# The middle query slot of a head pair: its two 64-query halves alternate, and with float32 scores it becomes one product

## The chip, the cores and the metric

The kernel runs on one NeuronCore of one Trainium2 chip. The metric is device time in microseconds (us) of one execution; of the kernel before, three runs are known: 794.02, 794.14 and 795.17 us, median 794.14 us. One more execution was taken by the hardware profiler, and everything said here of stretches, waits and instructions comes from that trace.

## The reference

Attention over 4 batches, 8 heads, 576 positions and head dimension 64, followed by a token-mixing block and a gated block on the result seen as (4, 576, 512):

```
scores = q @ k.T / 8                     # per batch and head, 576 x 576
scores = where(scores >= rowmax - tau, scores, -1e9)
attn   = softmax(scores)
x      = attn @ v                        # heads side by side: (4, 576, 512)
u      = x + (relu(x.T @ w_tok1) @ w_tok2).T
x      = u + relu(u @ w_ch1) @ w_ch2
h      = relu(x @ w_in);  c = conv3(h) along the sequence
out    = (h * sigmoid(c)) @ w_out
```

## The kernel before, in words

The heads are taken in pairs, `NP` = 4 pairs in each of the four batches. The two heads of a pair lie on the two halves of the 128 partitions: head 0's 64 head dimensions on partitions 0 to 63, head 1's on 64 to 127. The 576 queries of a head are four blocks of 128 and a rest of 64, so a pair has `NSL` = 9 slots of 128 queries: slots 0 to 3 are head 0's blocks, slots 5 to 8 head 1's, and slot 4, the middle one, holds the last 64 queries of both heads. `cut(slot)` says so: for the middle slot it gives two parts of 64 output partitions each, (0, 64, head 0) and (64, 64, head 1); for every other slot one part of 128.

`prep` loads a pair, `scores` makes a slot's scores on TensorE (PE) into one of two or three PSUM places, `exps`, `mask`, `ph` and `rest` run the row maximum, the exponential, the threshold and the split into a high and a low float16 half on VectorE (DVE), ScalarE (ACT) and GpSimd (POOL), a DMA transpose issued from SyncE (SP) turns the probabilities, and `pv` multiplies them with the values: per part nine key blocks `j`, each with the high half of v, and for `j` up to 4 also with the low half, hence 14 products of 65 or 64 columns per part. The middle slot has two parts, so 28 products, and in them only 64 of the 128 array columns are used (the profile writes 128*64).

The scores come in two kinds. In batches 0 and 1 (`NB32` = 2) they are float32 products: the queries `qt` stand as weights, and the keys stream through. There are two key tiles per pair, `kt[0]` and `kt[1]`, each with zeros on the other head's partitions, so that the contraction over 128 partitions sees one head. A slot is two products of 288 columns (the halves `a` of the keys); the middle slot is four, two for each head. In batches 2 and 3 the scores are float16 products of split operands, two passes `x` for each `a`.

The work is written as generators that step in turn: `attention(b + 1)` is woven between the products of `dense(b)` (token mixing is `tok`; L547, L565, L598, L621 and L624 are the dense products). Batch 0's attention has nothing dense to lie beside. A scheduler that runs when the program is built then places the instructions of every engine in a fixed order, by its own estimate of durations, so an edit can move instructions far from it. Each engine, and the SP queue of DMA issues, works through its own order and waits at semaphores.

Names in the rows: `ps` is PSUM, `pt` and `act_t` hold the transposed probabilities, `vh` and `vl` the halves of v, `wc`, `wi`, `wo` weights, `st` staged weights, `ld` loaded v.

Of the kernel before, what the change touches and what calls it, by code (L numbers as in the profile page):

```python
# [9 lines left out]
F16 = mybir.dt.float16  # L10
# [9 lines left out]
def kernel(ctx: ExitStack, tc: tile.TileContext, q, k, v, tau,  # L20
# [7 lines left out]
    nc = tc.nc  # L28
    B, NPR, _, S = q.shape
    H, D = 2 * NPR, 64  # L30
    P = 128
# [7 lines left out]
    NS = S // P  # L39
    R0 = NS * P  # L40
    SPL = [(0, 256), (256, S - 256)]
    NB32 = 2
# [12 lines left out]
    const = ctx.enter_context(tc.tile_pool(name="const", bufs=1))  # L55
# [10 lines left out]
    V, A, G, T = nc.vector, nc.scalar, nc.gpsimd, nc.tensor  # L66
# [41 lines left out]
    def hold(x):  # L108
        return tc.issue_after(turn[behind[x]].ins) if behind.get(x) in turn else nullcontext()
# [93 lines left out]
    for t in h_t:  # L203
# [2 lines left out]
    v_t = [(const.tile([P, 2, 2 * NS + 1, D + 2], F16, name=f"vh{i}"),  # L206
            const.tile([P, 2, NS + 1, D], F16, name=f"vl{i}")) for i in range(2)]
    qk_t = [(const.tile([P, 2, S], F16, name=f"qt{i}"),
             [const.tile([P, 2, S], F16, name=f"kt{i}_{h}") for h in range(2)]) for i in range(2)]

    def f32(t):
        return t.rearrange("p a s -> p (a s)").bitcast(F32)
# [10 lines left out]
    NSL = 2 * NS + 1  # L223

    def split(out, t, sc):
        A.activation(out=out[:, 0], in_=t, func=AF.Copy, scale=sc)
        V.scalar_tensor_tensor(out=out[:, 1], in0=t, scalar=sc, in1=out[:, 0], op0=ALU.mult, op1=ALU.subtract)

    def prep(b, p):

        vh, vl = v_t[p % 2]
        qt, kt = qk_t[p % 2]
        pair[b, p] = dict(qt=qt, kt=kt, vh=vh, vl=vl)
        if b < NB32:
            with hold("qk") if b else nullcontext():
                nc.sync.dma_start(f32(qt), q[b, p])
                for h in range(2):
                    if b == 0 and p < 2:
                        G.memset(f32(kt[h])[(1 - h) * D:(2 - h) * D], 0.0)
                    nc.sync.dma_start(f32(kt[h])[h * D:(h + 1) * D], k[b, p, h * D:(h + 1) * D])  # L240
            if b:
                yield
                yield
            A.activation(out=f32(qt), in_=f32(qt), func=AF.Copy, scale=qsc[:, 0:1])
        else:
            qn, kn = [qk2.tile([P, S], F32, tag="x", name="ld", bufs=15) for _ in range(2)]
            with hold("qk"):
                nc.sync.dma_start(qn, q[b, p])
                nc.sync.dma_start(kn, k[b, p])
        if b >= NB32:  # L250
            yield
            qs = qk2.tile([P, 2, S], F16, tag="x", name="qs", bufs=15)
            split(qs, qn, qsc[:, 1:2])
            for h in range(2):
                for x in range(2):
                    nc.sync.dma_start(qt[x * D:(x + 1) * D, h], qs[h * D:(h + 1) * D, x])
            yield
            ks = qk2.tile([P, 2, S], F16, tag="x", name="ks", bufs=15)
            split(ks, kn, QK)
            for h in range(2):  # L260
                for r in range(2):
                    nc.sync.dma_start(kt[h][r * D:(r + 1) * D], ks[h * D:(h + 1) * D])
        yield
        vn = []
        for hh in range(2):
            t = qk2.tile([P, S], F32, tag="x", name="ld", bufs=15)
            with hold("qk") if b else nullcontext():
                nc.sync.dma_start(t, v[b, 2 * p + hh])
            vn.append(t.rearrange("p (a d) -> p a d", d=D))
        yield  # L270
        for hh in range(2):
            G.tensor_scalar(out=vn[hh], in0=vn[hh], scalar1=VSC, scalar2=1.0, op0=ALU.mult, op1=ALU.mult)
            A.activation(out=vh[:, hh, :, 0:D], in_=vn[hh], func=AF.Copy)
            G.tensor_tensor(out=vl[:, hh], in0=vn[hh][:, 0:NS + 1], in1=vh[:, hh, 0:NS + 1, 0:D], op=ALU.subtract)
            yield

    def cut(slot):

        if slot == NS:
            return [(0, 64, 0, R0), (64, 64, 1, R0)]  # L280
        return [(0, P, 0, slot * P) if slot < NS else (0, P, 1, (slot - NS - 1) * P)]
# [4 lines left out]
    pair, chk, done = {}, {}, set()  # L286
    ps = psum.tile([P, 8, 512], F32, name="ps")
    hn = S // 2
# [8 lines left out]
    def where(i):  # L297
        return i // PER, i // NSL % NP, i % NSL

    def scores(i):  # L300
        b, p, slot = where(i)
        st = pair[b, p]
        o2 = 2 * (i % 3 if i < PER else i % 2)
        s3 = ps[:, o2:o2 + 2, :hn]
        for o, m, hh, q0 in cut(slot):
            for a in range(2):
                if b < NB32:
                    T.matmul(s3[o:o + m, a], f32(st["qt"])[:, q0:q0 + m],  # L308
                             f32(st["kt"][hh])[:, a * hn:(a + 1) * hn], start=True, stop=True)
                    continue  # L310
                for x in range(2):
                    T.matmul(s3[o:o + m, a], st["qt"][:, hh, q0:q0 + m],  # L312
                             st["kt"][hh][:, x, a * hn:(a + 1) * hn], start=(x == 0), stop=(x == 1))
        chk[i] = dict(s3=s3)

    def half(i, x):
# [42 lines left out]
    def pv(i):  # L359
        b, p, slot = where(i)  # L360
        st = pair[b, p]
        vh, vl, pt = st["vh"], st["vl"], chk.pop(i)["pt"]
        n = slot if slot <= NS else slot - NS - 1
        dst = ps[:, 7, n * (D + 1):(n + 1) * (D + 1)]
        for o, m, hh, _ in cut(slot):
            for j in range(NSL):
                T.matmul(dst[o:o + m], pt[:, j, o:o + m], vh[:, hh, j, 0:D + 1],  # L367
                         start=(j == 0), stop=(j == NSL - 1))
                if j <= NS:
                    T.matmul(dst[o:o + m, 0:D], pt[:, j, o:o + m], vl[:, hh, j], start=False, stop=False)  # L370
        if slot == 0:
            st["x32"] = p2.tile([P, NS + 1, P], F32, tag="x32", name="x32", bufs=1)
            st["xp"] = [p2.tile([P, NS + 1, P], F16, tag=f"x{x}", name=f"x{x}") for x in "hl"]
        if slot in (NS, NSL - 1):
            norm(ps[:, 7], st["x32"], st["xp"], 0 if slot == NS else 1)

    def norm(pvt, x32, xp, hh):


        n = NS + 1 - hh  # L380
        p3v = pvt[:, :n * (D + 1)].rearrange("p (a d) -> p a d", d=D + 1)
        rc = sm.tile([P, NS + 1, 1], F32, tag="rc", name="rc")
        V.tensor_scalar(out=rc[:, :n], in0=p3v[:, :, D:D + 1], scalar1=1e-9 * ONE, scalar2=None, op0=ALU.add)
        V.reciprocal(out=rc[:, :n], in_=rc[:, :n])
        cs = slice(hh * D, (hh + 1) * D)
        parts = [(slice(0, NS), cs)]
        V.tensor_tensor(out=x32[:, 0:NS, cs], in0=p3v[:, 0:NS, 0:D],
                        in1=rc[:, 0:NS].to_broadcast([P, NS, D]), op=ALU.mult)
        if hh == 0:
            V.scalar_tensor_tensor(out=x32[:, NS].rearrange("p (h d) -> p h d", h=2),  # L390
                                   in0=p3v[:, NS:NS + 1, 0:D].to_broadcast([P, 2, D]), scalar=rc[:, NS],
                                   in1=blk.to_broadcast([P, 2, D]), op0=ALU.mult, op1=ALU.mult)
            parts.append((slice(NS, NS + 1), slice(0, P)))
        for ss, cc in parts:
            A.activation(out=xp[0][:, ss, cc], in_=x32[:, ss, cc], func=AF.Copy)
            G.tensor_tensor(out=xp[1][:, ss, cc], in0=x32[:, ss, cc], in1=xp[0][:, ss, cc], op=ALU.subtract)
# [54 lines left out]
    def attention(b):  # L451
# [9 lines left out]
        for i in range(c0, c1, NSL):  # L461
            bb, p, _ = where(i + NSL)
            if bb < B:
                start(i - 1, prep(bb, p), (1, 2, 2, 1, 1, 1))
            start(i + NSL - 1 + lag + 2, tok(b, where(i)[1]), (2, 1, 1))
        if b == 0:
            for _ in prep(0, 0):
                pass
        i = c0 - 1
        while i < c1 + lag or todo:  # L470
            if c0 <= i < c1:
                exps(i)
            yield
            if c0 <= i - 1 < c1:
                mask(i - 1)
                ph(i - 1)
                if i == PER:
                    free.append(5)
            yield
            if c0 <= i - lag < c1:  # L480
                pv(i - lag)
            if c0 <= i - 1 < c1:
                rest(i - 1)
            for j in range(i + 1, i + (3 if i + 2 < PER else 2)):
                if j < c1 and j not in done:
                    scores(j)
                    done.add(j)
            yield
            for g in todo.pop(i, ()):
                next(g, None)  # L490
            yield
            i += 1
# [235 lines left out]
```

## Time and profile before

| what | value |
|---|---|
| median of three runs | 794.14 us |
| span of the profiled execution, first to last instruction | 783.1 us |
| what lies around the span (median less span) | 11.0 us |
| PE busy | 731.0 us, 93% of the span |
| DVE / ACT / POOL busy | 493.8 / 471.3 / 423.0 us |
| granted PE clock, mean | 0.997 of full speed |

No time of the profiled execution other than its span is known; the runs' median stands in for it. A busy share of PE counts products that overlap in the array as one busy stretch, so the share alone does not tell how far PE is from its limit; the start of one product to the start of the next does. Rows of the timeline give the start, the duration until the result is out, the shape and a count; consecutive products of one line are merged, and "128*64" means that 64 array columns are in use.

### The profile page before, as it was taken

How to read it: one execution, taken by the hardware profiler on the slowest of the kernel's cores; microseconds unless marked ns; L12 is line 12 of the kernel's file. 1: busy time of each engine (PE TensorE's matmuls, PEld its weight loads, DVE VectorE, ACT ScalarE, POOL GpSimd, SP SyncE). 2: the span in 40 equal slices, each digit the busy share in tenths (PEclk: the TensorE clock that was granted, in tenths of full speed). 3: DMA queues.
4: the chain of work that ended last, by engine and by line, in shares of the span. 5: the costliest groups of instructions: out<-in, count | busy, mean ns of one | idle time of the engine just before them, and what ended most of it. 6: DMA issues, size and time to landing. Idle time of an engine off the chain costs nothing. (4 is left out here: it accounts for less than half of the span.)

```text
span 783.1 us, 18470 instructions
## 1 busy us (share of the span) xinstructions
PE 731.0 (93%) x7388; PEld 554.2 (71%) x7388; DVE 493.8 (63%) x837; ACT 471.3 (60%) x998; POOL 423.0 (54%) x471
## 2 busy tenths in 40 slices
PE   5679978999987899999999999999999999999998
PEld 3457756778766675788887856788888756878764
DVE  5578876877677861666877980676876850323370
ACT  7789967876667762666656852676656741311371
POOL 5988889887786651355664950366564830000040
PEclk9999999999999999999999999999999999999999
DMA  8999998997987421668667412667664401000001
GB/s 282 187 241 189 173 233 190 215 245 204 229 212 171 89 35 42 142 146 159 130 142 156 84 40 76 127 144 156 146 129 76 77 15 48 1 1 2 1 1 61
DMA packets 195046, 97.84 MB, mean 125 GB/s; under 512 B 174096, under 2 KB 176656, under 8 KB 194960
## 3 DMA queue, kind: packets, MB, share of 16 engines
q1 hardware_dynamic: 194640, 96.39, 55.3%
q8 instruction: 58, 0.95, 0.5%
q10 hardware_dynamic: 320, 0.26, 0.1%
q14 instruction: 28, 0.23, 0.1%
HBM read 42.36 MB, written 4.72 MB: 60 GB/s over the span
## 5 line engine op out<-in xcount | busy, mean ns | idle before, releaser
L352 POOL TENSOR_TENSOR ph<-e,ph 128x576 f16<-128x576 f32 x108 | 141.3, 1308 | 94.3 <-ACT ph L348 87.4
L565 PE MATMUL ps<-act_t,wc_h 128*128 128x256 f16 (+1 forms) x768 | 149.0, 286 | 0.0
L324 DVE TENSOR_REDUCE nm<-ps 128x1 f32<-128x576 f32 x144 | 107.9, 752 | 44.1 <-PE ps L312 27.0
L588 POOL TENSOR_TENSOR act_t<-ct,act_t 128x576 f16<-128x576 f32 x32 | 46.6, 1456 | 138.8 <-ACT act_t L587 135.9
L547 PE MATMUL ps<-u_h,wc_h 128*128 128x256 f16 (+1 forms) x384 | 109.7, 286 | 0.8 <-DVE act_t L522 0.8
L565 PE MATMUL ps<-act_t,wc_l 128*128 128x256 f16 (+1 forms) x384 | 109.8, 286 | 0.0
L547 PE MATMUL ps<-u_h,wc_l 128*128 128x256 f16 (+1 forms) x384 | 109.6, 286 | 0.0
L547 PE MATMUL ps<-u_l,wc_h 128*128 128x256 f16 (+1 forms) x384 | 109.2, 286 | 0.0
L308 PE MATMUL ps<-kt,qt 128*128 128x288 f32 (+1 forms) x320 | 87.8, 433 | 18.6 <-DVE act_t L343 9.0
L343 DVE SCALAR_TENSOR_TENSOR e<-ps,thr,e 128x576 f32<-128x576 f32 x108 | 87.8, 813 | 21.1 <-POOL thr L332 9.4
L547 PEld LDWEIGHTS <-wc_h 128*128 128x128 f16 x768 | 75.1, 98 | 19.9 <-issue 1.3
L565 PEld LDWEIGHTS <-wc_h 128*128 128x128 f16 x768 | 74.9, 98 | 19.0 <-issue 0.5
L367 PE MATMUL ps<-vh,pt 128*128 128x65 f16 (+1 forms) x1080 | 71.9, 195 | 8.5 <-DMA pt<-ph 5.8
L598 PE MATMUL ps<-u_h,wi_h 128*128 128x256 f16 (+1 forms) x256 | 73.0, 286 | 6.4 <-ACT h L574 3.3
L583 DVE SCALAR_TENSOR_TENSOR ct<-h,cw,ct 128x576 f32<-128x576 f32 x64 | 68.4, 1069 | 14.8 <-ACT ct L581 14.3
L621 PE MATMUL ps<-wo_h,act_t 128*128 128x512 f16 x256 | 76.3, 379 | 1.5 <-DVE u_l L430 0.9
L367 PEld LDWEIGHTS <-pt 128*128 128x128 f16 (+1 forms) x1080 | 62.4, 101 | 18.3 <-DMA pt<-ph 10.2
L308 PEld LDWEIGHTS ps<-kt,qt 128*128 128x128 f32 (+1 forms) x320 | 50.5, 185 | 33.8 <-DVE act_t L343 12.7
L348 ACT ACTIVATE ph<-e 128x576 f16<-128x576 f32 x108 | 73.0, 676 | 2.1 <-DVE e L343 2.1
L598 PE MATMUL ps<-u_h,wi_l 128*128 128x256 f16 (+1 forms) x256 | 73.1, 286 | 0.0
L598 PE MATMUL ps<-u_l,wi_h 128*128 128x256 f16 (+1 forms) x256 | 73.1, 286 | 0.0
L621 PEld LDWEIGHTS <-act_t 128*128 128x128 f16 x384 | 36.7, 98 | 43.6 <-issue 1.7
(113 smaller groups left out, 1613.0 us busy)
## 6 DMA issues: line engine op xcount, KB each, us to landing
st<-in_moe_w_ch_dram SPq DMA_DIRECT2D x24, 512.0 KB, 4.3
ld<-in_v_dram SPq DMA_DIRECT2D x32, 288.0 KB, 3.6
kt<-ks SPq DMA_DIRECT2D x32, 144.0 KB, 2.7
st<-in_moe_w_in_dram SPq DMA_DIRECT2D x8, 512.0 KB, 4.7
st<-in_moe_w_out_dram SPq DMA_DIRECT2D x8, 512.0 KB, 4.5
out_dram<-ot SPq DMA_DIRECT2D x16, 256.0 KB, 2.0
qt<-in_q_dram SPq DMA_DIRECT2D x8, 288.0 KB, 3.6
kt<-in_k_dram SPq DMA_DIRECT2D x16, 144.0 KB, 3.7
```

Source lines behind the costliest of these rows:

```text
L308: T.matmul(s3[o:o + m, a], f32(st["qt"])[:, q0:q0 + m], f32(st["kt"][hh])[:, a * hn:(a + 1) * hn], start=True, stop=True)
L324: crit["max"] = V.tensor_reduce(out=nm, in_=c["s3"], axis=AX.XY, op=ALU.max, negate=True)
L343: crit["mask"] = V.scalar_tensor_tensor(out=e3, in0=c["s3"], scalar=c["thr"], in1=e3, op0=ALU.is_ge, op1=ALU.mult)
L348: A.activation(out=c["ph"][:, 0:S], in_=c["e"], func=AF.Copy)
L352: G.tensor_tensor(out=c["ph"][:, S:], in0=c["e"], in1=c["ph"][:, 0:S], op=ALU.subtract)
L367: T.matmul(dst[o:o + m], pt[:, j, o:o + m], vh[:, hh, j, 0:D + 1], start=(j == 0), stop=(j == NSL - 1))
L547: T.matmul(t, wc1[wx][:, f, c], u[c][ux][:, sl], start=(c == 0 and i == 0), stop=(c == NC - 1 and i == 2))
L565: T.matmul(t, wc2[wx][:, c, f], r_t(f, rx)[:, sl], start=(by_dve(c) and f == 0 and i == 0), stop=(f == NF - 1 and i == 2))
L583: V.scalar_tensor_tensor(out=ct, in0=ht[:, kk:kk + S], scalar=cw[:, kk, f:f + 1], in1=ct, op0=ALU.mult, op1=ALU.add)
L588: G.tensor_tensor(out=g_t(f, 1), in0=ct, in1=g_t(f, 0), op=ALU.subtract)
L598: T.matmul(t, wi[wx][:, f, c], u[c][ux][:, s0:s0 + n], start=(c == 0 and i == 0), stop=(c == NC - 1 and i == 2))
L621: T.matmul(t, g_t(f, gx)[:, j * P:(j + 1) * P], wo[wx][:, f], **lim)
```

## The change

In the middle slot the products of the two halves alternate: in `pv` the loop over the parts moves inside the loop over `j`, and in the float16 branch of `scores` inside the loops over `a` and `x`. For float32 scores the roles are exchanged: the zeros now lie in two query tiles `kts[:, h]`, held side by side, the keys lie whole in `qt`, and a slot is a window of 128 columns over the two query tiles. Head 1's queries are stored rotated, its last 64 first, so the window of slot 4 covers the last 64 queries of both heads, and the slot is two products of 128 columns instead of four of 64. The rotation makes head 1's query load two DMAs instead of one.

```diff
-             [const.tile([P, 2, S], F16, name=f"kt{i}_{h}") for h in range(2)]) for i in range(2)]
+             const.tile([P, 2, 2, S], F16, name=f"kt{i}")) for i in range(2)]
 ...
             with hold("qk") if b else nullcontext():
-                nc.sync.dma_start(f32(qt), q[b, p])
+                nc.sync.dma_start(f32(qt), k[b, p])
                 for h in range(2):
                     if b == 0 and p < 2:
                         G.memset(f32(kt[h])[(1 - h) * D:(2 - h) * D], 0.0)
-                    nc.sync.dma_start(f32(kt[h])[h * D:(h + 1) * D], k[b, p, h * D:(h + 1) * D])
+                nc.sync.dma_start(f32(kt[0])[0:D], q[b, p, 0:D])
+                nc.sync.dma_start(f32(kt[1])[D:P, S - R0:S], q[b, p, D:P, 0:R0])
+                nc.sync.dma_start(f32(kt[1])[D:P, 0:S - R0], q[b, p, D:P, R0:S])
 ...
-        for o, m, hh, q0 in cut(slot):
+        if b < NB32:
+            qs = f32(st["kts"].rearrange("p h x s -> p (h x) s"))[:, slot * P:(slot + 1) * P]
             for a in range(2):
-                if b < NB32:
-                    T.matmul(s3[o:o + m, a], f32(st["qt"])[:, q0:q0 + m],
-                             f32(st["kt"][hh])[:, a * hn:(a + 1) * hn], start=True, stop=True)
-                    continue
+                T.matmul(s3[:, a], qs, f32(st["qt"])[:, a * hn:(a + 1) * hn], start=True, stop=True)
+        else:
+            for a in range(2):
                 for x in range(2):
-                    T.matmul(s3[o:o + m, a], st["qt"][:, hh, q0:q0 + m],
-                             st["kt"][hh][:, x, a * hn:(a + 1) * hn], start=(x == 0), stop=(x == 1))
+                    for o, m, hh, q0 in cut(slot):
+                        T.matmul(s3[o:o + m, a], st["qt"][:, hh, q0:q0 + m],
+                                 st["kt"][hh][:, x, a * hn:(a + 1) * hn], start=(x == 0), stop=(x == 1))
 ...
-        for o, m, hh, _ in cut(slot):
-            for j in range(NSL):
+        for j in range(NSL):
+            for o, m, hh, _ in cut(slot):
                 T.matmul(dst[o:o + m], pt[:, j, o:o + m], vh[:, hh, j, 0:D + 1],
                          start=(j == 0), stop=(j == NSL - 1))
-                if j <= NS:
+            if j <= NS:
+                for o, m, hh, _ in cut(slot):
                     T.matmul(dst[o:o + m, 0:D], pt[:, j, o:o + m], vl[:, hh, j], start=False, stop=False)
```

The scheduler's order, at three places. First PE, at the `pv` products of the middle slot of batch 0's first pair (before, the point where head 0's part ends and head 1's begins; `vh` high half, `vl` low half):

```order
L367 MATMUL ps<-vh_153,act_t 64x65
L367 LDWEIGHTS act_t
L367 MATMUL ps<-vh_153,act_t 64x65
L367 LDWEIGHTS act_t
L367 MATMUL ps<-vh_153,act_t 64x65
L370 LDWEIGHTS act_t
L370 MATMUL ps<-vl_154,act_t 64x64
```

and the beginning of the same slot now:

```order
L373 LDWEIGHTS act_t
L373 MATMUL ps<-vh_153,act_t 64x65
L373 LDWEIGHTS act_t
L373 MATMUL ps<-vh_153,act_t 64x65
L377 LDWEIGHTS act_t
L377 MATMUL ps<-vl_154,act_t 64x64
L377 LDWEIGHTS act_t
L377 MATMUL ps<-vl_154,act_t 64x64
```

Before, all 14 products of one head stand ahead of the other's 14; now each product of head 0 is followed by head 1's.

Second PE again, at the `pv` products of the middle slot of batch 2's second pair, which lie between dense products (`wc` weights). Before:

```order
L565 MATMUL ps<-act_t,wc_h 128x320
L367 LDWEIGHTS pt
L367 MATMUL ps<-vh_155,pt 64x65
L370 LDWEIGHTS pt
L370 MATMUL ps<-vl_156,pt 64x64
```

and now:

```order
L572 MATMUL ps<-act_t,wc_h 128x320
L373 LDWEIGHTS pt
L373 MATMUL ps<-vh_155,pt 64x65
L318 LDWEIGHTS qt_157
L318 MATMUL ps<-kt_158,qt_157 128x288
L318 LDWEIGHTS qt_157
L318 MATMUL ps<-kt_158,qt_157 128x288
L318 LDWEIGHTS qt_157
L318 MATMUL ps<-kt_158,qt_157 128x288
L318 LDWEIGHTS qt_157
L318 MATMUL ps<-kt_158,qt_157 128x288
L373 LDWEIGHTS pt
```

Here four full-width score products of another slot have moved in behind the first 64-column product, so the slot is visited in two pieces. Over the whole program the `pv` products of middle slots stand in 21 pieces before and in 25 now, the float16 middle scores in 10 before and 11 now, and the 8 float32 ones in 8 before and in none now.

Third SP, the queue of DMA issues, from the v loads at the start of the program. Before:

```order
L268 DMA ld<-in_v_dram 128x576 x8
L357 DMA_TRANSPOSE act_t<-act_t 128x9x128
L118 DMA st<-in_moe_w_tok_dram 128x576 x2
L357 DMA_TRANSPOSE act_t<-act_t 128x9x128
L240 DMA kt_0_158<-in_k_dram 64x576
L236 DMA qt_157<-in_q_dram 128x576
L357 DMA_TRANSPOSE act_t<-act_t 128x9x128
```

and now:

```order
L273 DMA ld<-in_v_dram 128x576 x8
L243 DMA kt_158<-in_q_dram 64x576
L118 DMA st<-in_moe_w_tok_dram 128x576
L363 DMA_TRANSPOSE act_t<-act_t 128x9x128
L118 DMA st<-in_moe_w_tok_dram 128x576
L363 DMA_TRANSPOSE act_t<-act_t 128x9x128 x2
L118 DMA st<-in_moe_w_tok_dram 128x576
L239 DMA qt_157<-in_k_dram 128x576
L244 DMA kt_158<-in_q_dram 64x512
L245 DMA kt_158<-in_q_dram 64x64
```

The third pair's first load, which waits for PE's scores of the first pair's middle slot, has moved ahead of the first transpose, and the load that waits for the first pair's last slot has moved behind the third. Each of the eight float32 pairs has one load more. From batch 2 on SP's order of loads and transposes is the same as before.

## Rows read from the trace of the kernel before

**Rows 1.** Windows: busy us (count) of PE, PEld, DVE, ACT, POOL; clock, DMA share, GB/s.

```profile
0.00:125.00 125.00, 96.23 (x1082) 72.10 (x1083) 92.83 (x180) 101.00 (x217) 100.99 (x117) 0.99 0.98 220
125.00:280.00 155.00, 140.13 (x1409) 108.98 (x1409) 118.70 (x199) 112.50 (x236) 122.64 (x130) 1.00 0.80 186
280.00:620.00 340.00, 337.23 (x3634) 261.67 (x3633) 225.83 (x367) 204.38 (x439) 176.01 (x209) 1.00 0.54 113
```

**Rows 2.** Windows of 20 us, the same columns.

```profile
440.00:460.00 20.00, 18.40 (x252) 15.57 (x252) 18.43 (x25) 15.31 (x34) 17.24 (x16) 1.00 0.45 69
620.00:640.00 20.00, 18.43 (x192) 12.55 (x191) 14.58 (x19) 12.08 (x24) 9.74 (x9) 1.00 0.14 27
```

**Rows 3.** Waits of PE from 125 to 280 us: total us, times, longest.

```profile
PE ps L367 <- DMA pt<-ph: 3.1, 5, 1.0
```

**Rows 4.** Timeline of PE, one middle slot's pv products and what follows.

```profile
353.30 0.22 PE L367 MATMUL ps<-vh,pt 128*64 128x65 f16 x1
353.35 0.20 PE L370 MATMUL ps<-vl,pt 128*64 128x64 f16 x1
...
353.64 0.23 PE L367 MATMUL ps<-vh,pt 128*64 128x65 f16 x3
353.70 0.20 PE L370 MATMUL ps<-vl,pt 128*64 128x64 f16 x1
353.70 0.23 PE L367 MATMUL ps<-vh,pt 128*64 128x65 f16 x3
353.76 0.20 PE L370 MATMUL ps<-vl,pt 128*64 128x64 f16 x1
...
353.98 0.29 PE L367 MATMUL ps<-vh,pt 128*64 128x65 f16 x4
354.21 0.28 PE L547 MATMUL ps<-u_h,wc_h 128*128 128x256 f16 x1
354.32 0.27 PE L547 MATMUL ps<-u_h,wc_l 128*128 128x256 f16 x1
```

**Rows 5.** Timeline of PE, the output projection's 48 half-width products.

```profile
311.65 0.41 PE L624 MATMUL ps<-wo_h,act_t 128*64 128x256 f16 x4
...
314.19 0.28 PE L624 MATMUL ps<-wo_l,act_t 128*64 128x256 f16 x2
```

**Rows 6.** Timeline of PE, float32 scores: three whole slots, then a middle slot.

```profile
66.86 3.15 PE L308 MATMUL ps<-kt,qt 128*128 128x288 f32 x12
69.85 0.19 PE L367 MATMUL ps<-vh,act_t 128*128 128x65 f16 x1
...
150.44 1.20 PE L308 MATMUL ps<-kt,qt 128*64 128x288 f32 x8
151.56 0.31 PE L547 MATMUL ps<-u_h,wc_h 128*128 128x320 f16 x1
```

**Rows 7.** Timeline of PE, a middle slot's float16 scores.

```profile
358.60 0.69 PE L312 MATMUL ps<-kt,qt 128*64 128x288 f16 x8
359.22 0.28 PE L547 MATMUL ps<-u_h,wc_l 128*128 128x256 f16 x1
```

**Rows 8.** Timeline of PE, a piece of two half-width products between whole ones.

```profile
173.28 0.30 PE L547 MATMUL ps<-u_l,wc_h 128*128 128x320 f16 x1
173.51 0.25 PE L367 MATMUL ps<-vh,pt 128*64 128x65 f16 x2
173.69 0.99 PE L308 MATMUL ps<-kt,qt 128*128 128x288 f32 x3
```

**Rows 9.** Timeline of SP: start and duration of DMA issues.

```profile
15.35 1.65 SPq L357 DMA_TRANSPOSE act_t<-act_t  x1
...
20.88 0.55 SPq L240 DMA_DIRECT2D kt<-in_k_dram  x1
24.46 0.34 SPq L236 DMA_DIRECT2D qt<-in_q_dram  x1
```

**Rows 10.** Waits of SP's queue from 15 to 125 us: total us, times, longest.

```profile
SPq L357 <- POOL act_t L352: 14.0, 13, 2.4
```

More of the change, by code (lines that the diff above doesn't have):

```diff
@@ L231, in prep @@
         vh, vl = v_t[p % 2]
-        qt, kt = qk_t[p % 2]
-        pair[b, p] = dict(qt=qt, kt=kt, vh=vh, vl=vl)
+        qt, kts = qk_t[p % 2]
+        kt = [kts[:, h] for h in range(2)]
+        pair[b, p] = dict(qt=qt, kt=kt, kts=kts, vh=vh, vl=vl)
         if b < NB32:
             with hold("qk") if b else nullcontext():
-                nc.sync.dma_start(f32(qt), q[b, p])
+                nc.sync.dma_start(f32(qt), k[b, p])
                 for h in range(2):
```

## The prediction

> **What bounds the kernel now.** I read the windows first, to see where PE is the limit. Up to 125 us, batch 0's attention, PE is busy 96.2 of 125 us, while the DMA engines stand at a share of 0.98 and ACT and POOL at 101 us each: PE is not the limit. From 125 to 280 us (batch 1's attention inside the first dense block) PE is busy 140.1 of 155 us, with POOL at 122.6: mixed. From 280 to 620 us (batches 2 and 3's attention inside the dense blocks) PE is busy 337.2 of 340 us, and no other engine passes 226: there a product less is time less [rows 1]. Two stretches near this one are exceptions: from 440 to 460 and from 620 to 640 us PE is busy 18.4 of 20 us [rows 2], so the middle slots there, one of batch 2 and the last of batch 3, save little. That leaves six of the eight middle slots of these batches on a full PE. After 640 us the attention is over and nothing changes.
>
> Then I read the timeline of PE at the places that the diff touches, for the step from start to start, since a busy share hides how products overlap.
>
> **The pv products.** In one middle slot head 0's first ten steps take 0.29 us after the second start (353.35 to 353.64, nine steps), 0.032 us each. The slot is 28 products and runs from 353.30 to the next product at 354.21, 0.91 us; the row at 353.98 holds the last four, so the last starts at about 354.08, 0.78 us after the first. In one place the two heads overlap: where head 0 ends and head 1 begins, eight starts fall between 353.64 and 353.76, 0.12 us, 0.017 us a step [rows 4]. So the engine does run the two halves of the array beside each other, but only for the few products that it sees at the border. What alternation does is in the trace too: the output projection's half-width products (L624) already alternate. 46 of them start in 2.54 us (311.65 to 314.19), 0.110 us a pair [rows 5], and a full-width product of 256 columns also steps by 0.11 us (354.21 to 354.32) [rows 4]. So a pair of halves costs what one costs. For pv this makes 14 pairs: 0.05 us for the first step and 12 times 0.032, 0.43 us from first to last start in place of 0.78. The saving is 0.35 us a slot. Bounds: 0.35 by rows 5; by the border's 0.017 us, 27 steps are 0.46 and the saving is 0.32; if the overlap doesn't last, none. I take 0.35, the row with a sustained alternation.
>
> A rule speaks against it. The Trainium skill, "TensorE: Matmul & The Clock Gate", section "Wait — 56ns, not 53.3ns?", says that start-to-start never falls below about 25 ns however few columns a matmul has. By it a slot would be 27 times 0.025, an estimate of 0.68 us, the saving 0.1, and the whole sum about 793.4 us. The 0.017 us at the border [rows 4] lies under that floor, so I give the rule's case less weight than the forecast; it stands beside the rival "no overlap".
>
> **The float32 middle score.** Three whole slots of four instructions take 2.99 us to the next product (66.86 to 69.85), 1.00 us each. The middle slot, eight half-width instructions, takes 1.12 us (150.44 to 151.56) [rows 6]: its halves overlap already, and half the instructions are not half the time. What is left is the visit: going from whole to half-width and back. A piece of two half-width products stands between a product at 173.28 and one at 173.69, 0.41 us, of which about 0.13 is the step of the first and 0.06 the two products: a visit costs 0.22 us [rows 8]. The middle slot's 0.12 us holds the way back, and the way in adds about 0.1. I take 0.2 us saved per slot (bounds 0.12 and 0.22), four in batch 0 and four in batch 1.
>
> **The float16 middle score.** Eight products take 0.62 us to the next [rows 7]. They overlap too. If the second head starts when the first is two products ahead at most, alternation saves some 0.03 us; I take 0.03 (bounds 0 and 0.1), eight slots, 0.24 us.
>
> **More pieces.** The order now visits the half-width products in more pieces. On the full PE it is three more: two pv slots of batches 2 and 3 whose first product stands alone ahead of four whole score products, and one float16 score. At 0.22 us they give back 0.66 us. In batch 1 it is one more, 0.22 us.
>
> **The loads.** A pair with float32 scores has four loads for three. An issue stands 0.55 us on SP's queue at 20.88 us [rows 9], so eight pairs cost between nothing, if SP has time, and 8 times 0.55, 4.4 us, if SP paces the stage; six of the eight lie in the first 125 us, 3.3 us. The third pair's first load now stands ahead of the first transpose (15.35 us) and waits for PE's middle score; behind it are the transposes, and behind these pv's first products. In return the load that went out at 24.46 us, held by PE's last slot, no longer stands ahead of the third transpose. The bytes are the same. SP's own longest sum of waits here is for POOL, 14.0 us in 13 waits [rows 10], so SP is mostly not the pacer, and I take little: 1 us lost in batch 0. The same stage has PE savings of 4 times 0.35 and 4 times 0.2, 2.2 us, behind other engines; I take 1 us of it, and the stage's sum is 0, between 2.2 us less and 3.3 us more. The copy that scales the tile, the clears of the zero halves and the number of scaled elements stay as they were.
>
> **The sum.** Batches 2 and 3: six times 0.35 is 2.1, and 0.24, less 0.66: 1.7 us saved. Batch 1: four times 0.35 and four times 0.2, less 0.22, is 2.0 us of PE work. PE has 15 us idle of 155 there, and five of its waits, 3.1 us, are for the transposes that feed these very slots [rows 3], so a shorter slot often only lengthens the next wait; I take half, 1.0 us (bounds 0 and 2.0). Batch 0: 0. Together 2.7 us. The span of the profiled execution, 783.1 us, becomes 780.4; the 11.0 us around it stay, which gives 791.4 us against the median of 794.14.
>
> **The rivals.**
>
> *No overlap in pv.* Products of 65 columns may be handed out too fast to keep both halves fed, and a slot stays at 0.78 us. For it: the overlap at the border lasts only eight starts, and the sustained one is of products four times as long. Against: those eight starts. Then batches 2 and 3 lose 0.66 less 0.24, 0.4 us, batch 1 wins half of 0.8 less 0.22, 0.3: 794.2 us, no change.
>
> *The whole saving passes.* Batch 1's PE work counts in full (2.0) and batch 0's too (2.2, no load in the way), with 1.7: 5.9 us, 788.2 us. For it: the float32 scores feed the row maximum that frees the next PSUM place, so a shorter PE slot shortens that circle. Against: POOL and the DMA engines at rows 1.
>
> *SP paces the first 280 us.* Place: SP's queue, with one load more per pair and one ahead of the first transpose. Price: eight loads at 0.55, 4.4 us, and 0.55 us more ahead of the first transpose, 5.0 us; the transposes come later by as much, so batch 1's saving turns into waits for them. With 1.7 us won later it is 3.3 us slower: 797.4 us. It decides from 3.3 us lost, six loads, on. For it: the DMA share of 0.98; against: SP's waits for POOL.
>
> **How the numbers follow.** Forecast 0.56 (its own range 789.6 to 793.2), whole saving 0.14, no overlap 0.17, SP 0.13. A measurement of this kernel tells no change from one of 0.2%, 1.6 us: below 792.55 is faster, above 795.7 slower. The forecast's own range lies 0.83 below the line: 0.46, and with 0.14 that gives faster 0.60. The rest of the forecast, 0.10, and 0.16 of "no overlap" are the same, 0.26. SP's 0.13 and 0.01 from the middle cases are slower, 0.14. The scheduler has moved rows in all the first 280 us, and no row prices this; the range takes it in: 788.0 us, the whole saving, to 795.3, past "no overlap" and a third of the way to SP's case.
>
> **What would show it.** In the changed profile a middle slot's pv products should run 0.45 us or less from first to last start, in pairs of starts a few ns apart, and no float32 score row should be 128*64, each slot at 1.00 us. Right: PE still full from 280 to 620 us, the end of batch 3's attention earlier by about 2.7 us, and the time to the end of batch 0's attention within 1 us of before. Wrong: a pv slot at 0.7 us or more (the handing out binds); the first transpose 2 us later and never caught up (SP); or PE idle where it was full, the saving turned into waits for transposes or DVE.

## The result, and the profile after

The changed kernel takes 802.63 us (median of 4 runs, 801.55 to 805.6) against 794.52 us for the kernel before on the same chip: ratio 1.0129, 95% interval 1.0099 to 1.0159. It is slower; the forecast was 791.4 us, its range ended at 795.3. (The two medians alone give 1.0102; here and below the ratio is the recorded one, with its interval.)

First a correction to the table ahead of the prediction. In every later profile a run's time is its span and 1.8 us (after: 803.8 and 805.6). By that the profiled execution of before, with a span of 783.1 us, was one of some 785 us and lay at the fast end: before's runs in the experiments go from 784.58 to 795.36. Of the 11.0 us "around the span" only 1.8 are there. No term of the sum hangs on them, but stage times of that one profile are early by several us, so a second profile of before (first experiment, span 792.0) stands beside it below.

What the diff does in PE's products came out as worked out. In the timeline of the changed kernel, a middle slot's `pv` products and what follows, as in [rows 4]:

```profile
374.17 0.22 PE L373 MATMUL ps<-vh,pt 128*64 128x65 f16 x2
374.22 0.20 PE L377 MATMUL ps<-vl,pt 128*64 128x64 f16 x2
374.25 0.20 PE L373 MATMUL ps<-vh,pt 128*64 128x65 f16 x2
...
374.51 0.29 PE L373 MATMUL ps<-vh,pt 128*64 128x65 f16 x8
374.73 0.28 PE L554 MATMUL ps<-u_h,wc_h 128*128 128x256 f16 x1
374.85 0.27 PE L554 MATMUL ps<-u_h,wc_l 128*128 128x256 f16 x1
```

The halves start in pairs (x2). From the first product to the dense product behind the slot it is 0.56 us (374.17 to 374.73) where it was 0.91: 0.35 us less, the forecast's number. From first to last start seven of the nine undivided slots of 28 take 437 to 439 ns (780 to 782 in all of before's). The other two take 488 and 730 ns; PE is at half clock in part of the first and in all of the second.

The float32 middle slot is now a whole slot, 1.05 us from start to next (before 1.12, [rows 6]), and the float16 one takes 0.62 us as before [rows 7]:

```profile
150.93 1.21 PE L313 MATMUL ps<-qt,kt 128*128 128x288 f32 x4
151.98 0.30 PE L554 MATMUL ps<-u_h,wc_h 128*128 128x320 f16 x1
...
379.12 0.68 PE L318 MATMUL ps<-kt,qt 128*64 128x288 f16 x8
379.74 0.28 PE L554 MATMUL ps<-u_h,wc_l 128*128 128x256 f16 x1
```

The loss is elsewhere. SP's timeline of the changed kernel, to be held against [rows 9]:

```profile
9.63 7.78 SPq L273 DMA_DIRECT2D ld<-in_v_dram  x8
17.51 0.47 SPq L243 DMA_DIRECT2D kt<-in_q_dram  x1
18.09 0.52 SPq L118 DMA_DIRECT2D st<-in_moe_w_tok_dram  x1
18.70 1.61 SPq L363 DMA_TRANSPOSE act_t<-act_t  x1
```

The first transpose is issued at 18.70 us, before at 15.35 (16.19 in the second profile). Four more issues stand ahead of it: one more query load in each of the first two pairs, the third pair's first load, and a weight load. The windows of [rows 1] now:

```profile
0.00:125.00 125.00, 93.28 (x988) 69.82 (x989) 87.25 (x170) 94.34 (x203) 95.16 (x110) 0.90 0.98 202
125.00:280.00 155.00, 137.74 (x1324) 106.19 (x1323) 108.90 (x188) 104.55 (x218) 113.49 (x124) 0.98 0.82 193
280.00:620.00 340.00, 330.27 (x3520) 252.70 (x3519) 224.34 (x363) 200.76 (x433) 174.72 (x207) 0.99 0.56 112
```

In the first 125 us all engines do less than in [rows 1] (ACT 94.34 us for 101.00, POOL 95.16 for 100.99), and PE's mean granted clock is 0.90 of full speed for 0.99. But the second profile of before does hardly more in that window, so most of this difference is spread between executions of one kernel:

```profile
0.00:125.00 125.00, 93.03 (x1021) 68.91 (x1022) 89.00 (x173) 96.66 (x206) 96.40 (x112) 0.96 0.98 209
125.00:280.00 155.00, 142.25 (x1378) 110.21 (x1377) 115.13 (x193) 111.29 (x230) 121.35 (x129) 0.97 0.83 191
```

From 125 to 280 us the changed kernel's engines are behind both profiles of before, and its third window is less full because batch 1's stage now reaches into it. Its waits of PE for transposes (total us, times, longest), up to 125 us and from 125 to 280 us:

```profile
PE ps L373 <- DMA act_t<-act_t: 11.2, 11, 4.4
...
PE ps L373 <- DMA pt<-ph: 5.7, 8, 1.9
```

In the second profile of before the first of these rows is:

```profile
PE ps L367 <- DMA act_t<-act_t: 10.8, 11, 2.1
```

So up to 125 us the total is hardly larger than in that execution of before; what is new is one wait of 4.4 us, to which the end of the section on the experiments comes back. From 125 to 280 us the total is 5.7 us for 3.1 and 2.8 in the two profiles of before, so there the transposes come late, as a rival foresaw. But with the order kept, the fastest kernel of all, it is 4.6 us: these sums do not show what the waits cost.

By stages, us from the span's start to the first dense product and then by dense block, read from starts of products. A block ends at the start of its last whole product of the output projection (L621 before); block 0 holds batch 1's attention, block 1 batch 2's, block 2 batch 3's. It is one execution each: the same kernel differs by 4 us in the first two columns, so only the experiments' medians decide. The profiles of the changed kernel and the second one of before are of the slowest of their runs, 805.6 and 793.8 us.

| kernel | first dense product | block 0 | block 1 | block 2 | PE at half clock |
|---|---|---|---|---|---|
| before, profile given | 114.3 | 197.1 | 172.7 | 173.2 | 3.4 |
| before, second profile | 118.6 | 201.6 | 172.8 | 173.1 | 20.4 |
| after | 124.4 | 208.0 | 174.0 | 172.0 | 37.4 |
| order kept, halves alternate | 115.7 | 200.6 | 171.3 | 172.0 | 13.6 |
| new order, halves alternate | 118.6 | 205.7 | 173.2 | 173.8 | 23.8 |
| new order, halves in turn | 119.2 | 203.7 | 174.2 | 173.2 | 17.0 |

### The profile page after: what moved, and what is told of

It reads as the page before. It is cut to its first block, busy times and chain, and to the rows that moved or that the text cites. A ratio compares the mean times of both kernels' runs of the same rounds, so it can differ in the third digit from the quotient of the medians.

```text
span 803.8 us, 18420 instructions
## 1 busy us (share of the span) xinstructions
PE 739.5 (92%) x7356; PEld 557.8 (69%) x7356; DVE 496.0 (62%) x837; ACT 470.0 (58%) x998; POOL 422.7 (53%) x471
## 5 line engine op out<-in xcount | busy, mean ns | idle before, releaser
L313 PE MATMUL ps<-qt,kt 128*128 128x288 f32 x288 | 94.3, 460 | 22.8 <-DVE e L349 8.4
L554 PE MATMUL ps<-u_h,wc_h 128*128 128x320 f16 (+1 forms) x384 | 109.3, 286 | 0.3 <-DVE act_t L529 0.3
L554 PE MATMUL ps<-u_h,wc_l 128*128 128x320 f16 (+1 forms) x384 | 109.5, 286 | 0.0
L554 PE MATMUL ps<-u_l,wc_h 128*128 128x320 f16 (+1 forms) x384 | 108.7, 286 | 0.0
L313 PEld LDWEIGHTS ps<-qt,kt 128*128 128x128 f32 x288 | 55.0, 209 | 39.4 <-DVE act_t L349 10.5
L373 PE MATMUL ps<-vh,pt 128*128 128x65 f16 (+1 forms) x1080 | 69.0, 196 | 12.3 <-DMA pt<-ph 8.7
L373 PEld LDWEIGHTS <-pt 128*128 128x128 f16 (+1 forms) x1080 | 58.8, 102 | 20.6 <-DMA pt<-ph 12.3
L529 DVE SCALAR_TENSOR_TENSOR act_t<-ps,act_t 128x256 f16<-128x256 f32 (+1 forms) x96 | 43.1, 455 | 41.4 <-ACT act_t L528 40.7
```

The lines of the kernel that those rows point to most:

```text
L313: T.matmul(s3[:, a], qs, f32(st["qt"])[:, a * hn:(a + 1) * hn], start=True, stop=True)
L554: T.matmul(t, wc1[wx][:, f, c], u[c][ux][:, sl], start=(c == 0 and i == 0), stop=(c == NC - 1 and i == 2))
```

## The experiments

Three theories: **the loads** (the additional issues on SP ahead of the first transposes cost); **the order** (the scheduler, given other products or loads, makes another order of the whole program, and that order costs); **the products** (alternating products themselves disturb other engines). Ratios are to the kernel before on the same chip, with 95% intervals; before's median was 788.7 to 790.6 us in these sets of runs.

**The kernel before again**, no edit, for the spread of the measurement.

> The kernel before, unchanged, for a trace of its own on the chip that runs the others. Theory A (the stage before 125 us lost the time: loads on SP's queue, later transposes, and a PE so idle there that its clock is granted at half speed): the profiled span is nearer to 790 than to 783 us, with more than one stretch at half clock, so that part of the 20.7 us between the two profiles is the spread of the kernel before. Theory B (the whole difference is in the order of the changed kernel): span again near 783 us and one stretch at half clock.

789.87 us, 0.9987 (0.9955 to 1.0018). What is told of 0.5% below is told with its interval.

**Alternation alone**: `pv` and float16 scores by turns; float32 scores and loads as before.

```diff
-        for o, m, hh, _ in cut(slot):
-            for j in range(NSL):
+        for j in range(NSL):
+            for o, m, hh, _ in cut(slot):
 ...
```

> Alternation alone, in pv and in the float16 scores; the float32 scores and the loads as before. Theory A (loss from the float32 part): 0.2 to 0.5% faster than before, 790.5 to 793, pv slots at 0.44 us, the first transpose at 15 us. Theory B (the alternation spoils the order): slower by about 1%, 802.

798.61 us, 1.0101 (1.0051 to 1.0150). No load is added, the first transpose is issued at 15.85 us, and still most of the loss is there. The loads can't be the whole of it.

**Float32 scores alone**: zeros in the queries, one product, four loads; `pv` and float16 scores half after half.

```diff
-        for o, m, hh, q0 in cut(slot):
+        if b < NB32:
+            qs = f32(st["kts"].rearrange("p h x s -> p (h x) s"))[:, slot * P:(slot + 1) * P]
 ...
```

> The float32 part alone: zeros in the queries, one product for the middle slot, four loads a pair; pv and float16 scores by halves as before. Theory A: slower than before by 1.2 to 1.6%, 804 to 807, since it has the loss without the 2 us that the alternation saves; first transpose at 18 us or later, half clock in the first 60 us. Theory B: within 0.3% of before.

797.79 us, 1.0099 (1.0068 to 1.0130). Either half of the change costs about as much as the whole: not what two separate costs of parts would do.

**The kernel before with one load more**: head 1's keys in two pieces.

```diff
-                    nc.sync.dma_start(f32(kt[h])[h * D:(h + 1) * D], k[b, p, h * D:(h + 1) * D])
+                    cols = (slice(0, S),) if h == 0 else (slice(0, R0), slice(R0, S))
+                    for c in cols:
+                        nc.sync.dma_start(f32(kt[h])[h * D:(h + 1) * D, c], k[b, p, h * D:(h + 1) * D, c])
```

> The kernel before with one edit: head 1's key load is two loads (512 and 64 columns), as the changed kernel has for head 1's queries. Theory A1 (the additional load on SP's queue and the later transposes are the loss): slower by 0.7 to 1.5%, 800 to 806. Theory A2 (the exchange of roles and the one product are the loss, not the loads): within 0.3% of before, 792 to 797.

801.74 us, 1.0129 (1.0067 to 1.0190). No product is changed, the loss is that of the whole change, with the first transpose at 18.51 us. But the order on the other engines is new here too (of DVE's 837 instructions in the trace 734 stand in the same order, by operation, names and shapes), so this alone doesn't tell the loads from the order.

**The order kept**: the scheduler sees the kernel before; afterwards each run of half-width products on PE is put by turns (float32 middle scores too). Nothing else moves on any engine.

```diff
+def alternate(nc):
 ...
+            if i.opcode == "Ldweights" and tuple(i.tile_size) == (128, 64):
+                run[1 if i.tile_position[1] else 0].append((i, pe[k + 1]))
 ...
+    alternate(nc)
```

> The kernel before with the order that its scheduler made on every engine; only within each uninterrupted row of half-width products on PE (pv, float16 scores) are the two halves taken by turns, after scheduling. Theory O (the alternation saves its 0.35 us a slot, and what alternation alone lost in the last run is the new order that the scheduler made): 0.3 to 0.7% faster than before, 785 to 788.5 against 790.6. Theory W (a shorter pv slot only lengthens the next wait, or lets PE's clock fall more often): within 0.2% of before or slower.

786.36 us, 0.9951 (0.9929 to 0.9974). It beats both kernels. The theory of the products falls: the same alternation in the old order wins 0.49% of 790.55, 3.9 us. The order stands. Its timeline has the same short slot (a cut; 438 ns from first to last start):

```profile
358.24 0.22 PE L367 MATMUL ps<-vh,pt 128*64 128x65 f16 x2
...
358.59 0.29 PE L367 MATMUL ps<-vh,pt 128*64 128x65 f16 x8
```

**The changed kernel with one load for head 1's queries**, unrotated: head 1's scores then belong to other queries than the reference's.

```diff
-                nc.sync.dma_start(f32(kt[1])[D:P, S - R0:S], q[b, p, D:P, 0:R0])
-                nc.sync.dma_start(f32(kt[1])[D:P, 0:S - R0], q[b, p, D:P, R0:S])
+                nc.sync.dma_start(f32(kt[1])[D:P], q[b, p, D:P])
```

> The changed kernel, but head 1's queries come with one load, unrotated, so that head 1's scores belong to other queries than they should; as many loads as before. Its order on DVE, ACT, POOL and SP is that of the alternation alone, one instruction apart. Theory S (the additional load delays the first transposes and lengthens batch 0's attention): first transpose at 15 to 16 us, batch 0's attention ends near 118 us as in the kernel before, and the whole comes to 794 to 799, the alternation's 798.6 less up to 3 us for the eight single products. Theory R (the exchange of roles loses): 801 or more.

798.81 us, 1.0106 (1.0074 to 1.0138). Its order on DVE, ACT, POOL and SP is that of "alternation alone" but for one instruction, and so is its time: in this order the single float32 product is worth nothing that can be measured. It also ties the changed kernel's loss to the order: without the added load 1.0106 of its 1.0129 is left.

**The split key load for the first two pairs only, and for the others only.**

```diff
+                    cols = (slice(0, S),) if h == 0 or b or p > 1 else (slice(0, R0), slice(R0, S))
 ...
```

The second run has `h == 0 or not b and p < 2` in place of `h == 0 or b or p > 1`.

> The kernel before, with head 1's key load in two pieces for the first two pairs alone. Theory S: the first transpose at 18 us, batch 0's attention ends at 124 to 126 us as with all pairs split, 798 to 803 in all. Theory O (any new order loses, wherever the load stands): slower by about 1% too, but lost in another stage than batch 0's.

> The kernel before, with head 1's key load in two pieces for all float32 pairs but the first two. Theory S: first transpose at 15 to 16 us, batch 0's attention ends near 118 to 120 us, and the whole is within 0.4% of before (788 to 794). Theory O: slower by about 1%, 796 to 801.

First two pairs: 800.41 us, 1.0123 (1.0084 to 1.0162), first transpose at 18.01 us. The six others: 792.15 us, 1.0030 (1.0001 to 1.0058). The two loads at the start, with the order that they bring (742 of DVE's 837 instructions as before), make nearly the whole loss.

**The new order, halves in turn**: scheduled as "alternation alone", then put back half after half.

```diff
+            for pair in a + z:
+                out.extend(pair)
 ...
+    in_turn(nc)
```

> The scheduler's new order as in the kernel with alternation alone, but after the scheduler has run the half-width products are put back one half after the other, so that no two halves overlap except at the border; loads and float32 scores as before. With the kernel before, the one with the old order and alternation, and the one with the new order and alternation, this fills the fourth place of order against alternation. Theory O (the new order costs some 1.5%, the alternation gives back some 0.5% whichever order stands): ratio to before about 1.015, some 802 us, with a pv middle slot at about 0.78 us from first to last start. Theory A (it is the alternating slots themselves that disturb the first 280 us, by feeding later engines at other times): ratio 1.000, 790 us. A ratio of 1.010 or less would mean that in the new order the alternation gives nothing.

799.48 us, 1.0151 (1.0124 to 1.0179), and the undivided slots run 781 or 782 ns again. That closes the square of order against alternation: old order 1 and 0.9951, new order 1.0151 and 1.0101. The order costs 1.5% with either way of taking the halves (here the medians are 10.8 us apart). The alternation is worth 0.5% in the old order; in the new one the two figures point the same way, but their intervals overlap.

**The split load of the first two pairs, the small piece issued by ACT.**

```diff
-                        nc.sync.dma_start(f32(kt[h])[h * D:(h + 1) * D, c], k[b, p, h * D:(h + 1) * D, c])
+                        (A if c.start else nc.sync).dma_start(f32(kt[h])[h * D:(h + 1) * D, c], k[b, p, h * D:(h + 1) * D, c])
```

> The kernel before with head 1's key load of the first two pairs in two pieces, as in the earlier run that split only these, but the small piece of 64 columns is issued from ACT's queue, so that SP's queue has as many loads ahead of the first transpose as before. Theory S (what costs is the additional issue on SP ahead of the first transpose): first transpose below 16.5 us, end of batch 0's attention 118 us or earlier, ratio below 1.004. Theory O (what costs is the order that the scheduler makes anew once a load is added, wherever it is issued): ratio 1.008 to 1.015 with the first transpose as early as before.

789.35 us, 1.0000 (0.9972 to 1.0027), where the same piece on SP cost 1.2%. The first transpose is at 16.14 us; but the order is also nearer to before's (819 of DVE's 837 instructions, for 742 with the piece on SP). The pieces, bytes and products are the same in both; what costs is the place on SP and the order that it brings, and these two weren't parted.

**The changed kernel with the longer query piece issued by ACT.**

```diff
-                nc.sync.dma_start(f32(kt[1])[D:P, 0:S - R0], q[b, p, D:P, R0:S])
+                A.dma_start(f32(kt[1])[D:P, 0:S - R0], q[b, p, D:P, R0:S])
```

> The changed kernel with the longer of the two loads of head 1's queries issued from ACT's queue, so that SP has three loads for a pair, as before. Theory S (the load on SP is what the changed kernel loses): the first transpose back at about 16 us, 794 us or less, ratio 1.000 or below. Theory O (the order made anew): 797 to 802 us, ratio 1.008 to 1.013, with an early first transpose. A rival to both: ACT is itself busy over 100 of the first 125 us, so an issue there delays the exponentials, and the ratio stays above 1.013.

795.15 us, 1.0086 (1.0054 to 1.0118), first transpose at 16.77 us. Moving the load off SP gives back perhaps a third, and the intervals overlap. The larger part stays with the load off SP. That fits the order, which is new here too, but this run alone doesn't show it.

**The order kept up to about 337 us**: all slots alternate, but the scheduler sees the alternation of batches 2 and 3 alone; the slots of batches 0 and 1 are put by turns after it.

```diff
+        steps = [(j, c) for j in range(NSL) for c in cut(slot)] if b >= NB32 else [(j, c) for c in cut(slot) for j in range(NSL)]
 ...
```

> All half-width products of pv and of the scores alternate, as in the kernel whose order was kept, but only the slots of batches 0 and 1 are alternated after the scheduler has run; those of batches 2 and 3 already alternate when it schedules. Its order on DVE, ACT, POOL and SP is therefore that of the kernel before up to about 337 us and is made anew behind that. Theory E (the new order costs mainly where PE is not full, in the first 310 us): ratio 0.997 to 1.000, some 788 to 790 us: the gain of the order kept, less about 1.8 us each in the two blocks behind 300 us, as the stages of the earlier profiles put it. Theory L (the price is spread over the whole attention or sits in the later blocks): 1.003 or more. If nothing is lost at all, 0.995 as with the order kept throughout.

790.07 us, 0.9998 (0.9971 to 1.0024). Between the order kept (0.9951) and new throughout (1.0101): of the 1.5% some 0.5% is lost behind 337 us, and about 1%, 8 us, is lost ahead of it, where PE waits for others. The division is rough: the intervals of 0.9951 and 0.9998 just overlap.

**One place where the new order loses.** In the changed kernel PE stands still from 50.2 us, waiting for the eleventh transpose. The first row is PE's, the others SP's, which issued it at 48.12 us:

```profile
54.57 0.24 PE L373 MATMUL ps<-vh,act_t 128*128 128x65 f16 x1 [4.38 <-DMA act_t<-act_t]
...
46.51 0.33 SPq L118 DMA_DIRECT2D st<-in_moe_w_ch_dram  x1
46.90 0.48 SPq L243 DMA_DIRECT2D kt<-in_q_dram  x1
47.43 0.59 SPq L245 DMA_DIRECT2D kt<-in_q_dram  x1
48.12 3.91 SPq L363 DMA_TRANSPOSE act_t<-act_t  x2
```

With the order kept it is issued at 46.41 us, and PE's wait for it is 1.03 us:

```profile
51.15 0.20 PE L367 MATMUL ps<-vh,act_t 128*128 128x65 f16 x1 [1.03 <-DMA act_t<-act_t]
...
45.77 0.53 SPq L118 DMA_DIRECT2D st<-in_moe_w_ch_dram  x1
46.41 3.91 SPq L357 DMA_TRANSPOSE act_t<-act_t  x2
```

From issue to landing in the trace this transpose took 6.4 us in the changed kernel, and 5.9 to 7.3 us in all seven kernels with a ratio of 1.0099 or more. In the seven profiles of the others (two of before, and the runs from 0.9951 to 1.0086) it took 4.6 to 5.3 us. Two loads of queries more stand ahead of it in the changed kernel, but "alternation alone" has only the weight load there, and its wait is as long (4.68 us). So the long landing goes with the loss, and PE's wait at this place is some 3 us longer; that these 3 us reach the end of the program is not shown. In windows of one us, the columns of [rows 1], a packet counts where it starts. Those of the changed kernel that start from 52 to 53 us take 3.04 times the window of all 16 DMA engines, few start in the next, and PE's granted clock is 0.50:

```profile
52.00:53.00 1.00, 0.00 (x0) 0.00 (x0) 0.81 (x1) 0.29 (x1) 1.00 (x3) 0.50 3.04 160
53.00:54.00 1.00, 0.00 (x0) 0.00 (x0) 0.00 (x0) 0.00 (x0) 1.00 (x2) 0.50 0.19 33
```

Packet by packet the traces say more. In the changed kernel 17 packets of 256 bytes end together at 51.86 us after up to 1.64 us, and 27 more at 53.94 us after up to 1.41 us. Such a common stop (ten or more packets of 512 bytes or less, of 0.45 us or more each, that end together) falls into the eleventh transpose once to three times in each of the seven slower kernels, once in each of the two that issue a load from ACT, and never in the other five profiles. A profile has 28 to 35 of them whatever the kernel: the new order does not make more, it meets them elsewhere. In 315 of the 439 stops of all profiles a packet of the kind "instruction" starts in the 1.5 us before, a stretch that covers some 15% of the span. The two go together; whether one makes the other no run tells, and the place was not tested by itself.

## Why the prediction was wrong

**The products: right.** 0.35 us for a `pv` slot (measured 0.35), a whole float32 slot, 0.01 us for a float16 one where 0.03 was forecast. The floor of 25 ns a start that the Trainium skill states ("TensorE: Matmul & The Clock Gate", "Wait — 56ns, not 53.3ns?") does not hold here: 27 steps in 0.438 us are 16 ns each on average. The rival "no overlap" falls with it.

**Batches 2 and 3: right only with the order kept.** There block 1 is 1.5 us and block 2 is 1.1 us shorter than in the second profile of before, 2.6 us for a forecast of 2.3 without the extra pieces, which that order does not have. The total is 3.9 us (interval 2.1 to 5.6) for the 2.7 forecast. Batch 1's 1.0 us can't be read: block 0 differs by 4.5 us between the two profiles of before. In the changed kernel block 1 is 1.2 us longer and block 2 1.1 us shorter. The three extra pieces at 0.22 us were not the whole price of the new order on a full PE: some 3.7 us, with a wide interval, of the order's gain are lost again behind 337 us, from 0.9951 to 0.9998.

**The failed step: "the stage's sum is 0" for batch 0, and with it the price of nothing for the rest of the scheduler's moves up to 280 us.** The prediction said that the scheduler "has moved rows in all the first 280 us, and no row prices this", and then let the range take it in at less than 4 us, upward. It is the largest term: 1.5% in all, two thirds of it ahead of 337 us. I had weighed what each edit does at its own place; the scheduler answered either half of the change with a new interleaving of every engine, and before's order was the better one. Why it is better stays open but for the one wait above. And what is shown for the order is shown on "alternation alone"; the changed kernel's own order was not run with before's products, so there the order and the added loads are parted only as far as the run with one load goes (1.0106 of 1.0129).

**The rival on SP: the right sign, as far as the runs show the smaller part.** The first transpose is 3.35 us later (2.5 against the second profile), not 0.55: each of the two extra query loads, the third pair's load and a weight load add to one another ahead of it. In the changed kernel it isn't caught up (first dense product at 124.4 us for 118.6). But with "float32 scores alone" the first transpose is nearly as late, at 18.03 us, and the first dense product comes at 118.7: a late first transpose alone does not decide the stage. And the rival's point of decision, six loads at 0.55 us, was wrong: loads behind the first two pairs cost 0.3%, the two at the start 1.2%, and with the small pieces on ACT nothing, each in an order of its own.

**The float32 product: mis-sized.** 0.2 us a slot was forecast, bounds 0.12 and 0.22; 0.07 stands in the rows, since the whole slot takes 1.05 us there and not 1.00. In the whole kernel 1.0106 against 1.0101 shows no gain.

## What to carry to other kernels

When a scheduler orders the program, an edit is two changes: its own products and the order made anew; the second can be the larger. Here the order cost 1.5% and the alternation won 0.5%. Price it by a control before trusting a sum: apply the edit after scheduling, with the order kept, and run the new order with the old products. And count every issue that moves ahead of the first transfer on which the start depends, on the queue where it stands.

## What the hardware showed that I had not expected

- Alternating half-width products start every 16 ns on average (28 in 0.438 us), well below the 32 ns of one half alone [rows 4].
- A wait can cost twice, by the clock behind it: in the changed kernel PE stands still from 50.2 to 54.6 us, and its granted clock is half of full speed from 51.5 to 58.4 us. In all it is at half clock for 37.4 us of the span, 20.4 and 3.4 us in the two profiles of before. Two whole float32 slots, eight instructions, that start at 25.80 us at half clock last 4.19 us there; the same at full clock, in the profile of before, last 2.21 us:

```profile
25.80 4.19 PE L313 MATMUL ps<-qt,kt 128*128 128x288 f32 x8
```

```profile
58.47 2.21 PE L308 MATMUL ps<-kt,qt 128*128 128x288 f32 x8
```

- A transpose that lands in 4.6 us in one order lands in 7.3 us in another, with three common stops of packets in it, of 1.29, 0.61 and 1.44 us; in the 4.6 us there is none.
